# Sliding-window attention with sinks, then a gated feed-forward: half of the row-maximum shift at two places as the bias of the exponentials, the constants' load behind that of the first keys, and another order by hand

## The chip, the cores and the metric

The kernel runs on one core of a Trainium2 chip. The time is device microseconds for one execution. Five engines run their own instruction streams and wait for each other through semaphores: PE (TensorE, matrix products, with its weight loads shown as PEld), DVE (VectorE), ACT (ScalarE), POOL (GpSimd) and SP, which only issues DMAs here.

## What is computed

Attention over 4 batches, 8 heads, 768 positions, head size 64, followed by a feed-forward block on the 3072 tokens of 8 x 64 = 512 features. A query sees the 4 first keys (the sinks) and the 128 last ones.

```python
scores = scale * np.matmul(q, k.transpose(0, 1, 3, 2))
is_sink = pos[None, :] < 4
in_window = (rel >= 0) & (rel < 128)          # rel = query position - key position
scores = np.where(is_sink | in_window, scores, -1e9)
scores = scores - np.max(scores, axis=-1, keepdims=True)
a = np.exp(scores)
a = a / (np.sum(a, axis=-1, keepdims=True) + 1e-09)
attn = np.matmul(a, v)                         # then (B, S, H*D) = (3072, 512)
h = x @ w_in                                   # 512 -> 2048
g = h * (1.0 / (1.0 + np.exp(-1.702 * h)))
out = g @ w_out                                # 2048 -> 512
```

## The kernel before

**Tiles.** The 3072 tokens are 24 blocks of 128; block b belongs to batch b // 6. The blocks are worked on in the order ORDER, and the position of a block in it is its *place*: places 0 to 3 are the first blocks of the four batches (blocks 0, 6, 12, 18), which have no block before them and no sinks apart from their own keys; places 4 to 23 are the other 20. Two places make a *pair*; the feed-forward of a pair starts when both of its places are done.

**One place.** Its stages, with their lines:
- loads of queries, keys and values by POOL's DMA queue, which convert to 16 bits on the way (L255, L277, L284). The keys of place 0 alone are loaded raw by SP's queue (L263) and converted by an engine (`round16`, L266 to L271), because `CFG["hw"]` names them. A pair's queries and keys share one buffer of the ring `qkn` (4 buffers).
- transposes of queries and keys. Places 0 to 7: by PE into PSUM (`tq`, L398 and L405; for places 0 to 3 in 16 small products for each of the two, with the identity matrix out of the constants), evicted by DVE or ACT (L355, L359) into `qkT`. From place 8: by one DMA transpose for a pair (L433), issued by SP.
- scores. Places 0 to 3: a mask is written to PSUM by two products (L473, out of the constants), and the scores of the block with itself are added (L481). Later places: the scores with the own block, those with the block before (`prv`) and those with the sinks (L510); DVE copies the part of `prv` that is inside the window over the own scores (L527).
- row maximum (L537, and L554, L557 for the sinks), subtraction of it (L578, and L602 for the sinks) into `e`, and the exponential by ACT (L617) into `a`. At places 0 to 3 maximum, subtraction and exponential are done in two halves of four heads each ("fine").
- transpose of the probabilities. Places 0 to 5: by PE (`ta`, L657), evicted by DVE or ACT. From place 6: by a DMA transpose issued by SP (L682). Places 4 to 23: POOL then splits it in two by two selects (L620, L624), one for the own values and one for those of the block before.
- products with the values (`av`, L709 to L719), division by the sum (L726, L727), and the transpose of the result into `xT`: by PE at places 0 to 5 (`tx`, L745), by one DMA transpose a pair from place 6 (L758).

**Feed-forward of a pair.** `first` (L780): products with w_in into a PSUM buffer `hT`, eight of them. At the first pair, which is worked on a token block at a time, product u needs chunk u mod 4 of w_in; the gate there is a tanh by ACT (L794) and a product by DVE (L801), so that ACT doesn't have to change its table between it and the exponentials. All later pairs have the gate in one ACT instruction (L810). `second` (L834): the sum over 2048 features with w_out into PSUM; the result is evicted by ACT or DVE and written by SP's queue (L852).

**PSUM.** Rings of buffers: `mm` (3 banks; transposes, `hT`, the outputs, and part of `av`), `own` (scores, 2 banks), `pv` (2 banks; `prv`, `av`, and the own scores of places 1 and 3), `mi` (1 bank). A product can only start when a buffer of its ring has been read out.

**What sets the order.** Every operation is an entry of a plan, with engines that may take it, what it depends on, and the buffers that it takes and gives back. The order, and the engine of each operation, is not searched when the program is built: it is the string SEQUENCE, where `38d` says that entry 38 comes next and runs on DVE (p is PE, a ACT, d DVE, t POOL, s SP). Each engine executes its entries in this order and waits where an input or a buffer isn't there. The costs, transfer times and due times at the entries were used by the search that wrote the string; they don't act on the program. The entries are numbered as they are added. Numbers that the text needs: 0 load of the constants, 37 raw load of place 0's keys, 38 their conversion, 12 to 18 queries and keys of places 0 to 3, 19, 20, 23, 24 the values of places 0, 1, 2, 3, 21, 22, 25, 26 the chunks 0 to 3 of w_in, 101 to 123 place 0, 124 to 146 place 1, 147 to 169 place 2, 170 to 192 place 3 (in each: transposes and evictions first, then mask, scores, maxima, subtractions, exponentials), 197 the scores of place 4, 270, 296, 322, 348 the DMA transposes of queries and keys of places 8 and 9, 10 and 11, 12 and 13, 14 and 15.

The entry with the bias exists in the code before, for a place that `CFG["nb"]` names; before, it names none. With n halves named, the last n halves of the place get no subtraction:

```python
plan.add(DVE, ..., nc.vector.tensor_scalar(out=nbias[:, 2-nb:], in0=small[:, 2-nb:], scalar1=-scale, op0=ALU.mult))
for j in range(4):     # one ACT instruction of 128 columns for each head, straight from the scores in PSUM
    nc.scalar.activation(out=a16()[:, 512*l + P*j : 512*l + P*j + P], in_=own(l, l+1)[:, 0, j],
                         func=AF.Exp, scale=scale, bias=nbias[:, l, j : j + 1])
```

Of the kernel before, what the change touches and what calls it, by code (L numbers as in the profile page):

```python
# [27 lines left out]
PE, ACT, DVE, POOL, SP = "PE", "ACT", "DVE", "POOL", "SP"  # L28
# [1 line left out]
    tq=(0, 1, 2, 3, 4, 5, 6, 7),  # L30
    ta=(0, 1, 2, 3, 4, 5),
    tx=(0, 1, 2, 3, 4, 5),
    nb={},
    wide={1: 'pv', 3: 'pv'},
    fine=(0, 1, 2, 3),
    split=(0, 1),
    gbatch={},
    tanh=(0, 1),
    last=(256, 128, 128),
    hw=["k0"],  # L40
    big=(0, 1, 2, 3),
    avb={0: ("mi", "mm"), 1: ("mi", "mm"), 2: ("mi", "mm")},
    hb={},
# [11 lines left out]


SEQUENCE = """
0s 10d 4d 37s 12t 7d 14t 11a 16t 13t 106p 38d 15t 9d 2d 103p 6d 23t 3d 101p 104a 20t 126p 102a 18t 107p 127d 17t
124p 19t 108d 149p 109d 125a 22t 147p 150a 110d 129p 25t 148a 130p 111d 112a 105t 131d 113a 114p 132d 170p 115a 26t
116p 133d 171a 118p 152p 21t 117a 119d 153p 135a 134d 29t 120p 8d 137p 136a 121d 172p 33t 138a 154d 122p 173a 30t  # L60
139p 156d 123a 175p 155d 174t 140a 141p 481p 142d 158a 24t 157d 143p 176p 482a 144d 160p 34t 159a 483d 145p 161a 27t
177d 162p 484p 163a 146d 28t 179d 166p 487p 485a 167d 181a 486d 493p 488a 178d 489d 490p 40t 494a 180d 39t 478p 491a
495d 182a 32t 492d 183p 164p 479a 165d 499p 36t 184a 480d 185p 42t 500a 187p 195p 186d 193p 501d 48t 189p 196a 496p
190d 194a 168p 188d 497a 217p 215p 197p 169a 498d 218a 198p 191p 43t 199d 514p 192a 508p 216d 515a 200d 518p 46t
201d 509p 519a 31t 202d 239p 502p 240a 52t 203d 219p 128t 237p 221d 503p 238a 204a 520p 67t 222d 220p 510p 5d 223d
93s 504p 225d 224d 1s 242p 49t 94s 511p 151d 226a 45t 505p 512d 241p 521a 51t 506d 516p 243d 54t 524p 517a 244d 205p
525a 528p 206d 253p 245d 529a 255p 207t 522p 254d 247d 256a 246d 530p 35t 523a 227p 97t 208p 248a 228d 258p 257p
209d 270s 531p 259d 210t 230p 532p 260d 231a 229t 211p 261d 526p 249s 232t 212d 533p 527a 263d 262d 44t 233p 60t
536p 234d 264a 55t 213p 534d 537p 214d 41t 271p 538p 50t 273d 265s 235p 250t 539p 236a 274d 272p 548p 540a 296s 275d
550p 276d 57t 549a 552p 58t 277d 283p 53t 553a 544p 285d 551a 266t 554p 545a 286d 284p 251p 555a 287d 542p 61t 252d  # L70
546p 47t 288d 267p 56t 547a 556p 543a 268d 564p 289d 557a 269s 278a 558p 541s 297p 559p 299d 290a 565p 279s 300d
298p 566p 535s 301d 560p 96s 302d 291s 567p 303d 309p 304a 280t 95s 561p 311d 568a 305s 310p 578p 562d 570p 312d
579a 322s 292t 576p 98d 281p 571a 572p 66t 282d 584p 306t 313d 573a 507s 577a 513s 293p 585a 580p 294d 64t 574p 314d
581a 295s 84t 592p 575a 315d 316a 63t 307p 593p 59t 308d 586p 73t 317s 582p 72t 594p 99t 583a 587p 70t 323p 604p
325d 348s 595p 605a 326d 588p 596a 318t 324p 600p 327d 328d 589p 601a 598p 329d 65t 590d 335p 591s 78t 608p 563s
337d 62t 612p 609a 338d 69t 599a 336p 602p 613a 68t 339d 319p 603a 341d 340d 82t 606p 76t 620p 320d 607a 85t 342a
614p 100d 321s 79t 610p 361p 75t 330a 621p 343s 363d 91t 615p 611a 364d 331s 362p 616p 365d 622p 367d 366d 617p 623p
618a 632p 374s 624d 638p 636p 344t 639a 349p 637a 630p 351d 350p 626p 631a 352d 332t 345p 627a 634p 633a 346d 628p
353d 81t 640p 354d 629a 635a 333p 368a 648p 334d 642p 355d 347s 375p 356a 643p 569s 377d 641a 376p 357s 649p 378d
644p 369s 379d 650p 380d 645p 625s 656p 619s 646d 597s 381d 387p 358t 657a 400s 662p 389d 668p 663a 370t 651p 669a  # L80
359p 652a 388p 654p 360d 77t 658p 390d 74t 660p 659a 391d 80t 655a 371p 393d 392d 661a 71t 664p 372d 676p 665a 382a
373s 401p 670p 403d 647s 402p 671p 404d 394a 383s 666p 405d 677p 667a 406d 395s 672p 407d 413p 408a 673p 415d 384t
684p 674d 678p 416d 685a 409s 414p 679p 90t 417d 426s 692p 87t 680d 385p 418d 693a 396t 696p 419d 386d 686p 682p 88t
687a 397p 410t 683a 690p 697a 398d 688p 691a 399s 698p 689a 420a 694p 411p 699p 412d 695a 421s 700p 427p 675s 710p
429d 452s 712p 711a 430d 428p 701p 713a 422t 431d 720p 432d 724p 721a 702d 439p 725a 86t 433d 718p 441d 92t 716p
719a 442d 83t 440p 714p 717a 89t 423p 715a 732p 434a 424d 704p 443d 425s 445d 733p 444d 435s 722p 446a 705p 723a
681s 465p 447s 706p 467d 734p 703s 468d 466p 750p 436t 469d 735p 751a 470d 707p 736a 448t 742p 708a 746p 743a 437p
747a 738p 438d 748p 471d 739a 449p 749a 740p 472a 450d 744p 451s 453p 726p 745a 473s 455d 727p 456d 737s 454p 728p
741a 653s 457d 760p 459d 458d 752p 474t 729p 753a 460a 761p 730d 772p 762p 773a 461s 766p 763p 767a 780p 764a 770p
475p 462t 771a 768p 781a 476d 776p 769a 778p 777a 788p 779a 463p 774p 464d 782p 775a 477s 789p 765s 783p 731s 784p  # L90
790p 785p 796p 786d 791p 797a 754p 792a 808p 793s 709s 794p 787s 809a 802p 795a 755p 803a 806p 756p 807a 798p 800p
799a 757p 801a 804p 758d 822p 759s 805a 810p 816p 811p 823p 812p 824p 813p 817p 814a 825p 818p 826a 815s 828p 819p
827s 829p 820d 830p 831p 821s 832a 833a
"""


# [69 lines left out]
def kernel(  # L166
# [28 lines left out]
    plan = Plan(RING)  # L195
# [26 lines left out]
    def by(e):  # L222
        return nc.sync if e == SP else nc.scalar
# [19 lines left out]
    )  # L243

    def sw(key, cost, fn, xfer, **kw):
        return plan.add(POOL, key, cost, fn, xfer=xfer, post=0.9, **kw)

    ld, qkn = {}, {}

    def load_block(which, b, key, after=0.0):  # L250
        bb, r = divmod(b, 6)
        pair, i = divmod(PLACE[b], 2)
        src = {"q": q, "k": k, "v": v}[which][bb, :, r * P : (r + 1) * P, :].rearrange("h s d -> s h d")
        if which == "v":
            return sw(key, 0.88, lambda b=b, x=2: nc.gpsimd.dma_start(v65[:, b, :, 0:D], src), 0.88 if pair < 4 else 0.95, deps=[z_1], after=after)  # L255
        w = "qk".index(which)
        buf = qkn[pair]
        if which + str(PLACE[b]) in CFG["hw"]:
            raw = const.tile([P, H * D], FP32, name=f"raw_{which}{b}")
            n = CFG["hw"].index(which + str(PLACE[b]))  # L260
            src = {"q": q, "k": k}[which][bb, :, r * P : (r + 1) * P, :].rearrange("h (t e) d -> t h (e d)", e=8)
            got = plan.add(
                {SP: 0.45, ACT: 0.6}, -120 + n, 0, lambda e, src=src, raw=raw, x=9: by(e).dma_start(raw, src), xfer=0.75, post=0.6  # L263
            )

            def round16(e, b=b, w=w, i=i):  # L266
                dst, src = buf()[:, i, w].rearrange("p h d -> p (h d)"), raw
                if e == ACT:
                    nc.scalar.copy(out=dst, in_=src)
                else:  # L270
                    (nc.vector if e == DVE else nc.gpsimd).tensor_copy(out=dst, in_=src)  # L271

            return plan.add({DVE: 0.42, ACT: 0.6, POOL: 0.8}, -110 + n, 0, round16, deps=[got], take=[buf])
        if PLACE[b] in CFG["big"]:
            return sw(
                key, 0.64,
                lambda b=b, w=w, i=i: nc.gpsimd.dma_start(  # L277
                    buf()[:, i, w].rearrange("p h d -> p (h d)"),
                    {"q": q, "k": k}["qk"[w]][bb, :, r * P : (r + 1) * P, :].rearrange("h (t e) d -> t h (e d)", e=8),
                ),  # L280
                0.7, take=[buf], after=after,
            )
        return sw(
            key, 0.88, lambda b=b, w=w, i=i: nc.gpsimd.dma_start(buf()[:, i, w], src), 0.88 if pair < 4 else 0.95,  # L284
            take=[buf], after=after,
        )
# [4 lines left out]
    def load_w_in(f, key):  # L291
        def go(f=f, x=0):
            nc.gpsimd.dma_start(  # L293
                w_in16[:, :, bass.ts(f, 512)],
                moe_w_in.rearrange("(c p) f -> p c f", p=P)[:, :, bass.ts(f, 512)],
            )

        return sw(key, 0.8, go, 2.5)

    def load_w_out(f, key):  # L300
        def go(f=f, x=1):
            nc.gpsimd.dma_start(
                w_out16[:, bass.ts(f, 4)],
                moe_w_out[bass.ts(f, 512), :].rearrange("(c p) f -> p c f", p=P),
            )

        return sw(key, 0.8, go, 2.5)

    for n, what in enumerate(CFG["loads"]):
        w, x = what[0], int(what[1:])  # L310
        x = ORDER[x] if w in "qkv" else x
# [583 lines left out]
```

## Time and profile before

| | |
|---|---|
| runs | 229.1, 229.35, 229.35 us; median 229.35 |
| the profiled execution | 228.31 us, span from the first to the last instruction 226.6 us |
| granted TensorE clock | 1.00 in every stretch |
| busy | PE 214.5, ACT 136.6, DVE 136.2, POOL 113.5 us |
| DMA | 32.47 MB in 226.6 us |
| costliest lines | L780 (`first`) 94.1 us, L834 (`second`) 91.8 us, both PE |

Busy time of the engines by stretch, in us of the stretch:

| stretch | PE | DVE | ACT | POOL |
|---|---|---|---|---|
| 0 to 10 | 4.50 | 3.62 | 3.16 | 8.85 |
| 10 to 20 | 8.68 | 9.43 | 8.90 | 6.64 |
| 20 to 30 | 9.27 | 9.05 | 7.66 | 5.76 |
| 30 to 40 | 10.00 | 8.79 | 7.11 | 5.07 |
| 60 to 80 | 19.85 | 15.76 | 12.07 | 11.49 |
| 80 to 100 | 20.00 | 12.19 | 10.96 | 15.73 |
| 100 to 120 | 18.77 | 11.62 | 11.10 | 11.66 |
| 120 to 140 | 20.00 | 13.93 | 12.44 | 7.76 |
| 200 to 227 | 23.48 | 1.92 | 7.07 | 0.00 |

A group's line in the profile reads: code line, engine, operation, output and inputs, their shapes, the number of instructions; then busy time in us and the mean of one in ns; then the idle time of the engine just before them and what ended it. A line of the timeline reads: start, duration, engine, line, operation, and in brackets the idle time before it and what ended it.

### The profile page before, as it was taken

How to read it: one execution, taken by the hardware profiler on the slowest of the kernel's cores; microseconds unless marked ns; L12 is line 12 of the kernel's file. 1: busy time of each engine (PE TensorE's matmuls, PEld its weight loads, DVE VectorE, ACT ScalarE, POOL GpSimd, SP SyncE). 2: the span in 40 equal slices, each digit the busy share in tenths (PEclk: the TensorE clock that was granted, in tenths of full speed). 3: DMA queues.
4: the chain of work that ended last, by engine and by line, in shares of the span. 5: the costliest groups of instructions: out<-in, count | busy, mean ns of one | idle time of the engine just before them, and what ended most of it. 6: DMA issues, size and time to landing. Idle time of an engine off the chain costs nothing.

```text
span 226.6 us, 5625 instructions
## 1 busy us (share of the span) xinstructions
PE 214.5 (95%) x2378; PEld 151.7 (67%) x2378; DVE 136.2 (60%) x243; ACT 136.6 (60%) x190; POOL 113.5 (50%) x135
## 2 busy tenths in 40 slices
PE   1889899999999999999899999999999999999994
PEld 0658876776784785675675685686765956856763
DVE  0899898998896852796286677843957371111010
ACT  2588696796746766367349249848585669613511
POOL 8955654698980689397071670780816112300000
PEclk9999999999999999999999999999999999999999
DMA  6999999999999999999998998999998072042112
GB/s 128 174 205 196 178 191 191 156 142 137 134 164 157 203 210 156 120 219 134 148 174 133 260 138 144 127 147 130 150 116 198 4 191 38 17 138 77 66 46 93
DMA packets 123512, 32.47 MB, mean 143 GB/s; under 512 B 114880, under 2 KB 120416, under 8 KB 123488
## 3 DMA queue, kind: packets, MB, share of 16 engines
q0 software_dynamic: 71792, 13.51, 79.6%
q1 hardware_dynamic: 51552, 18.55, 44.7%
q8 instruction: 18, 0.29, 0.6%
q10 hardware_dynamic: 144, 0.07, 0.1%
q14 instruction: 6, 0.05, 0.1%
HBM read 27.46 MB, written 6.29 MB: 149 GB/s over the span
## 4 chain that ended last, share of the span: by engine, by line
PE 77%; DMA 10%; POOL 5%; DVE 2%; ACT 1%; SPq 1%; issue 1%; POOLq 0%; DVEq 0%
PE o L834 33%; PE hT L780 31%; DMA w_in<-in_moe_w_in_dram 6%; DMA at<-a 4%; PE own L481 3%; PE av L715 2%; PE av L719 2%; PE av L709 2%; PE prv L481 2%; POOL qkn L277 2%; SPq L682 1%; POOL v L255 1%; POOL w_in L293 1%; PE tq L405 1%; PE snk L510 1%
## 5 line engine op out<-in xcount | busy, mean ns | idle before, releaser
L780 PE MATMUL hT<-xT,w_in 128*128 128x256 f16 (+1 forms) x896 | 94.1, 257 | 1.4 <-DMA xT<-xn 0.6
L834 PE MATMUL o<-w_out,gT 128*128 128x512 f16 (+2 forms) x416 | 91.8, 363 | 0.0
L810 ACT ACTIVATE gT<-hT 128x512 f16<-128x512 f32 x88 | 50.9, 597 | 58.7 <-PE hT L780 58.4
L780 PEld LDWEIGHTS <-w_in 128*128 128x128 f16 x896 | 75.3, 98 | 14.5 <-DMA xT<-xn 1.1
L834 PEld LDWEIGHTS <-gT 128*128 128x128 f16 x416 | 37.2, 98 | 32.2
L620 POOL TENSOR_SCALAR_AFFINE_SELECT atp<-at 128x1024 f16<-128x1024 f16 (+1 forms) x22 | 22.2, 1009 | 65.7 <-DMA at<-a 64.7
L527 DVE COPY_PREDICATED own<-consts,prv 128x1024 f32<-128x1024 uint16 x20 | 24.6, 1229 | 24.3 <-PE prv L481 24.2
L537 DVE TENSOR_REDUCE mx<-own 128x8 f32<-128x1024 f32 (+1 forms) x28 | 29.7, 1068 | 0.9 <-PE own L481 0.4
L578 DVE TENSOR_TENSOR e<-own,mx 128x1024 f32<-128x1024 f32 (+1 forms) x28 | 29.8, 1066 | 0.9
L617 ACT ACTIVATE a<-e 128x1056 f16<-128x1056 f32 (+1 forms) x28 | 26.2, 952 | 4.9 <-issue 2.6
L624 POOL TENSOR_SCALAR_AFFINE_SELECT at<-at 128x1024 f16<-128x1024 f16 (+1 forms) x22 | 22.5, 1024 | 1.5
L355 DVE COPY osb<-o 128x512 f32<-128x512 f32 (+1 forms) x12 | 8.0, 666 | 24.3 <-PE o L834 24.3
L284 POOL DMA_DIRECT2D qkn<-in_k_dram x20 | 17.8, 902 | 7.4 <-DMA w_out<-in_moe_w_out_dram 5.1
L255 POOL DMA_DIRECT2D v<-in_v_dram x24 | 21.4, 902 | 0.0
L726 DVE RECIPROCAL rcp<-av 128x8 f32<-128x8 f32 (+1 forms) x28 | 5.5, 195 | 26.5 <-PE av L719 26.4
L284 POOL DMA_DIRECT2D qkn<-in_q_dram x20 | 17.8, 894 | 2.3 <-DMA qkn<-in_k_dram 0.7
L810 ACT ACT_TABLE_LOAD x14 | 18.0, 1283 | 0.2
L727 DVE TENSOR_TENSOR xn<-av,rcp 128x512 f16<-128x512 f32 (+1 forms) x28 | 17.2, 615 | 1.0
L715 PE MATMUL av<-v,at 128*128 128x65 f16 x192 | 17.0, 194 | 0.6 <-POOL at L624 0.5
L617 ACT ACT_TABLE_LOAD x13 | 16.7, 1283 | 0.2
L715 PEld LDWEIGHTS <-at 128*128 128x128 f16 x192 | 14.2, 98 | 2.5 <-POOL at L624 1.2
L481 PEld LDWEIGHTS <-qkT 64*128 64x128 f16 x352 | 10.2, 96 | 7.8 <-issue 5.1
(56 smaller groups left out, 165.9 us busy)
## 6 DMA issues: line engine op xcount, KB each, us to landing
out_dram<-osb SPq DMA_DIRECT2D x23, 256.0 KB, 2.5
qkn<-in_q_dram POOLq DMA_DIRECT2D x24, 128.0 KB, 5.3
v<-in_v_dram POOLq DMA_DIRECT2D x24, 128.0 KB, 5.6
qkn<-in_k_dram POOLq DMA_DIRECT2D x23, 128.0 KB, 8.6
w_in<-in_moe_w_in_dram POOLq DMA_DIRECT2D x4, 512.0 KB, 10.2
w_out<-in_moe_w_out_dram POOLq DMA_DIRECT2D x4, 512.0 KB, 11.6
at<-a SPq DMA_TRANSPOSE x18, 3.3
raw_k<-in_k_dram SPq DMA_DIRECT2D x1, 256.0 KB, 4.6
```

The source lines that it names most:

```text
L255: return sw(key, 0.88, lambda b=b, x=2: nc.gpsimd.dma_start(v65[:, b, :, 0:D], src), 0.88 if pair < 4 else 0.95, deps=[z_1], after=after)
L284: key, 0.88, lambda b=b, w=w, i=i: nc.gpsimd.dma_start(buf()[:, i, w], src), 0.88 if pair < 4 else 0.95,
L527: nc.vector.copy_predicated(out=own(lo, hi).rearrange("p l j s -> p (l j) s"), mask=later.unsqueeze(1).to_broadcast((P, 4 * (hi - lo), P)) ...
L537: lambda lo=lo, hi=hi, own=half, small=small: nc.vector.tensor_reduce(out=small[:, lo:hi], in_=own(lo, hi), axis=AX.X, op=ALU.max),
L578: nc.vector.tensor_tensor(out=e32()[:, 512 * lo : 512 * hi].rearrange("p (l j s) -> p l j s", j=4, s=P), in0=own(lo, hi), in1=small[:, lo: ...
L617: nc.scalar.activation(out=a16()[:, lo:hi], in_=e32()[:, lo:hi], func=AF.Exp, scale=scale)
L620: nc.gpsimd.affine_select(out=atp()[:, lo : lo + n], in_=at()[:, lo : lo + n], pattern=[[0, n], [-1, P]], compare_op=ALU.is_gt, fill=0.0, ...
L624: nc.gpsimd.affine_select(out=at()[:, lo : lo + n], in_=at()[:, lo : lo + n], pattern=[[0, n], [1, P]], compare_op=ALU.is_ge, fill=0.0, ba ...
L715: nc.tensor.matmul(acc[:, j], at()[:, c], v65[:, b, h], start=(r == 0), stop=(r == 0))
L780: nc.tensor.matmul(ht()[:, n], w_in16[:, c, bass.ts(f, P)], xt[g]()[:, tok, c], start=(c == 0), stop=(c == 3))
L810: lambda fs=fs, cols=cols, gt=gt, ht=ht: nc.scalar.activation(out=gt()[:, fs[0] : fs[-1] + 1, cols], in_=ht(), func=AF.Gelu_apprx_sigmoid),
L834: nc.tensor.matmul(po(), gt()[:, F, bass.ts(t, P)], w_out16[:, F, cols], start=(F == 0), stop=(F == NF - 1))
```

## The change

Four things:
- `CFG["nb"]` names places 2 and 3 with one half each. There, for the second half of the heads, the subtraction of the maximum by DVE (128x512) and the one exponential of 512 columns out of `e` become one DVE product of the four maxima with -scale and four exponentials of 128 columns each, out of PSUM, with that product as bias. The scores' PSUM buffer is given back by the exponentials. Entries 156 to 159 (place 2) and 179 to 182 (place 3) were: subtraction, subtraction, exponential, exponential; they are: product, subtraction of the first half, exponentials of the second half, exponential of the first half.
- SP's queue begins with the raw load of place 0's keys; the constants come second. Place 0's mask products come behind its transposes and not ahead of them.
- The whole string SEQUENCE is another one, and with it the engine of several operations.
- Costs, transfer times and due times of loads in the plan are changed. They are numbers of the search that wrote the string.

```diff
-    nb={},
+    nb={2: 1, 3: 1},
...
-    hw=["k0"],
+    hw=['k0'],
...
 SEQUENCE = """
-0s 10d 4d 37s 12t 7d 14t 11a 16t 13t 106p 38d 15t 9d 2d 103p 6d 23t 3d 101p 104a 20t 126p 102a 18t 107p 127d 17t
-124p 19t 108d 149p 109d 125a 22t 147p 150a 110d 129p 25t 148a 130p 111d 112a 105t 131d 113a 114p 132d 170p 115a 26t
-116p 133d 171a 118p 152p 21t 117a 119d 153p 135a 134d 29t 120p 8d 137p 136a 121d 172p 33t 138a 154d 122p 173a 30t
-139p 156d 123a 175p 155d 174t 140a 141p 481p 142d 158a 24t 157d 143p 176p 482a 144d 160p 34t 159a 483d 145p 161a 27t
-177d 162p 484p 163a 146d 28t 179d 166p 487p 485a 167d 181a 486d 493p 488a 178d 489d 490p 40t 494a 180d 39t 478p 491a
...
+37s 6d 0s 7d 12t 4d 16t 3d 15t 13t 10d 11a 14t 38a 17t 18t 103p 20t 101p 104a 19t 106p 102a 22t 107p 25t 124p 108d
+26t 126p 125a 8d 149p 109d 127a 21t 147p 110d 129p 148a 23t 111d 130p 150a 33t 2d 112a 131d 113a 114p 133d 105t 172p
+115a 132d 116p 152p 135a 30t 117d 173a 134d 120p 170p 29t 121d 118p 136a 137p 153p 119d 138a 139p 24t 154d 171a 122p
+141p 140a 155d 175p 151t 123a 143p 156d 176p 157d 481p 144d 158a 34t 142d 484p 177d 482a 145p 159a 9d 483d 146a 180d
+160p 485a 487p 27t 161d 182a 486d 128t 493p 178d 488a 162p 489d 494a 163d 28t 490p 495d 40t 179d 166p 164p 491a 478p
...
-        return plan.add(POOL, key, cost, fn, xfer=xfer, post=0.9, **kw)
+        return plan.add(POOL, key, cost, fn, xfer=xfer, **{"post": 1.1, **kw})
...
-                {SP: 0.45, ACT: 0.6}, -120 + n, 0, lambda e, src=src, raw=raw, x=9: by(e).dma_start(raw, src), xfer=0.75, post=0.6
+                {SP: 0.45, ACT: 0.6}, -120 + n, 0, lambda e, src=src, raw=raw, x=9: by(e).dma_start(raw, src), xfer=0.9, post=0.6
...
-                key, 0.64,
+                key, 0.56,
...
-        return sw(key, 0.8, go, 2.5)
+        return sw(key, 0.8, go, 2.5, post=2.0)
```

What the new string holds in the stretches that the prediction speaks of:

| where | before | after |
|---|---|---|
| POOL's first loads | queries of 0, keys of 1, keys of 2, queries of 1, queries of 2, values of 2, values of 1, keys and queries of 3, values of 0, then w_in chunks 1, 2, 3, 0 | queries of 0, keys and queries of 2, queries and keys of 1, queries and keys of 3, values of 1, values of 0, then w_in chunks 1, 2, 3, 0, then values of 2 |
| PE's first products | masks of 0, transposes of 0, keys of 1, scores of 0, queries of 1, transposes of 2, masks and scores of 1 | transposes of 0, masks and scores of 0, transposes of 1, transposes of 2, masks and scores of 1 |
| conversion of place 0's keys | DVE | ACT |
| ACT ahead of the first exponential | 5 evictions of queries and keys | the conversion and 6 evictions |
| evictions of `ta` of places 0, 2 and 3 | DVE has 1 of 6 | DVE has 5 of 6 |
| second copy of xT of place 1 | DVE | ACT |
| PE between `av` of place 7 and the first product of pair 3 (places 6 and 7) | 1 `first`, 2 `second`, scores of 10, 2 `second`, sinks, 3 `second`, scores of 11, 1 `second`, sinks | 2 `second`, scores of 10, 1 `first`, sinks, 3 `second` |
| PE between `av` of place 11 and the first product of pair 5 (places 10 and 11) | 1 `first`, 2 `second`, 1 `first`, scores of 15, 2 `second`, sinks, 4 `second` | 2 `second`, 1 `first`, 1 `second`, scores of 15, 1 `second`, sinks, 2 `second` |
| POOL between the selects of places 10 and 11 | 7 loads, one vsb product | 10 loads |
| POOL between the selects of places 11 and 13 | 11 loads | one copy of sink keys |

More of the change, by code (lines that the diff above doesn't have):

```diff
@@ L63 @@
[L63 to L92, printed above, removed]
@@ L93 @@
-827s 829p 820d 830p 831p 821s 832a 833a
+37s 6d 0s 7d 12t 4d 16t 3d 15t 13t 10d 11a 14t 38a 17t 18t 103p 20t 101p 104a 19t 106p 102a 22t 107p 25t 124p 108d
+26t 126p 125a 8d 149p 109d 127a 21t 147p 110d 129p 148a 23t 111d 130p 150a 33t 2d 112a 131d 113a 114p 133d 105t 172p
+115a 132d 116p 152p 135a 30t 117d 173a 134d 120p 170p 29t 121d 118p 136a 137p 153p 119d 138a 139p 24t 154d 171a 122p
+141p 140a 155d 175p 151t 123a 143p 156d 176p 157d 481p 144d 158a 34t 142d 484p 177d 482a 145p 159a 9d 483d 146a 180d
@@ new lines @@
+160p 485a 487p 27t 161d 182a 486d 128t 493p 178d 488a 162p 489d 494a 163d 28t 490p 495d 40t 179d 166p 164p 491a 478p
+167d 39t 181a 492d 183p 165d 32t 499p 479a 184d 36t 480d 185p 500a 187p 186d 195p 43t 193p 501d 189p 496p 194a 188d
+31t 196a 190d 217p 497a 215p 168p 197p 498d 169a 218a 199d 191p 514p 216a 42t 192a 200d 198p 508p 515a 518p 201d
+202d 509p 35t 519a 239p 48t 203d 237p 219p 240a 54t 220p 502p 238a 221d 204a 503p 222d 520p 46t 223d 504p 224d 510p
+225d 5d 241p 226a 93s 49t 511p 1s 521a 45t 505p 512d 73t 243d 242p 516p 506a 44t 524p 244d 517a 41t 205p 525a 528p
@@ new lines @@
+245d 206d 522p 529a 247d 246d 253p 523a 255p 530p 254d 61t 248a 256d 208p 207t 227p 270s 209d 257p 97d 531p 259d
+210t 228a 230p 532p 231a 260d 229t 258p 211p 249s 261d 526p 232t 212d 533p 527a 263d 262d 52t 233p 536p 55t 234d
+264a 213p 57t 537p 214d 51t 271p 538p 250t 273d 534a 265s 235p 539p 236a 274d 272p 548p 540a 53t 275d 552p 277d 549a
+62t 276d 296s 550p 283p 266t 553a 554p 285d 284p 542p 555a 94s 286d 551a 59t 251p 287d 544p 47t 252d 546p 58t 545a
+289d 543a 288d 267p 50t 547a 558p 278a 268d 564p 269s 297p 556p 299d 513s 298p 279s 565p 557a 300d 559p 541s 98t
@@ new lines @@
+301d 566p 507s 290a 302d 95s 60t 578p 303d 567p 304a 309p 291s 568d 280t 560p 311d 579a 305s 576p 312d 561p 577a
+281p 562a 322s 310p 570p 282d 292t 572p 313d 571a 314d 574p 65t 580p 315d 535s 575a 66t 293p 581a 584p 573a 306t
+294d 586p 585a 295s 316a 592p 74t 587p 90t 582p 64t 317s 307p 583a 69t 593p 308d 67t 588p 63t 323p 604p 70t 325d
+589p 56t 605a 326d 324p 594p 590a 79t 327d 612p 72t 328d 600p 318t 613a 335p 601a 595p 337d 348s 606p 174t 596a 329d
+338d 598p 607a 602p 336p 608p 603a 339d 599a 341d 319p 340d 609a 620p 330a 320d 614p 321s 610p 342a 615p 361p 611a
@@ new lines @@
+343s 621p 363d 362p 563s 622p 364d 591s 616p 331s 365d 638p 366d 374s 344t 617p 639a 367d 623p 618a 349p 75t 632p
+351d 597s 332t 628p 569s 633a 352d 624a 350p 634p 353d 345p 635a 84t 355d 630p 629a 346d 68t 636p 631a 88t 626p 85t
+333p 627a 91t 640p 637a 334d 78t 648p 354d 641a 347s 99t 642p 356a 81t 649p 76t 375p 650p 377d 368a 357s 643p 378d
+376p 651p 369s 379d 644p 380d 668p 625s 652d 387p 669a 619s 645p 389d 400s 358t 656p 646d 660p 657a 390d 658p 370t
+381d 662p 659a 359p 663a 83t 654p 360d 77t 664p 655a 71t 661a 388p 371p 391d 665a 82t 666p 382a 372d 670p 392d 373s
@@ new lines @@
+676p 393d 394a 401p 383s 671p 403d 667a 677p 395s 404d 402p 678p 405d 647s 672p 407d 96s 406d 679p 384t 673p 408a
+680d 413p 674d 684p 415d 396t 696p 685a 409s 416d 385p 414p 426s 686p 386d 690p 687a 397p 691a 410t 692p 697a 398d
+688p 417d 693a 399s 682p 419d 689a 418d 86t 411p 683a 80t 694p 412d 87t 698p 695a 100t 420a 427p 699p 429d 710p 430d
+700p 421s 711a 428p 701p 431d 681s 432d 716p 452s 702a 724p 439p 725a 422t 718p 717a 441d 675s 703s 712p 719a 433d
+442d 714p 713a 440p 720p 715a 443d 423p 721a 732p 434a 424d 704p 444d 722p 445d 435s 446a 733p 705p 723a 653s 425s
@@ new lines @@
+734p 465p 447s 706p 467d 436t 466p 726p 468d 735p 469d 707p 736a 471d 470d 437p 708a 448t 727p 709s 438d 746p 742p
+89t 747a 449p 92t 743a 728p 472a 450d 738p 451s 729p 739a 737s 453p 730d 473s 744p 455d 752p 745a 456d 750p 740p
+751a 454p 772p 741a 457d 753a 459d 474t 748p 458d 773a 778p 749a 760p 779a 460a 768p 761p 770p 461s 762p 771a 475p
+763p 476d 769a 766p 764a 774p 767a 776p 462t 775a 782p 777a 783p 780p 788p 781a 784p 463p 789p 464d 754p 477s 790p
+731s 785p 791p 786d 755p 792d 796p 756p 797a 802p 757p 803a 806p 758d 808p 759s 807a 793s 794p 809a 787s 765s 798p
@@ L94 @@
+795a 800p 799a 822p 801a 804p 823p 805a 810p 824p 811p 825p 816p 826d 812p 827a 817p 813p 818p 814a 828p 819p 815s
+829p 820d 830p 831p 821s 832a 833a
 """
@@ L305, in go @@
             )
-        return sw(key, 0.8, go, 2.5)
+        return sw(key, 0.8, go, 2.5, post=2.0)
     for n, what in enumerate(CFG["loads"]):
```

## The prediction

> **What bounds the kernel now.** I read the page's engine table first, then what PE waited for, then the timeline of the first 30 us, then PE's chain and SP's queue in the middle.
>
> ```profile
> span 226.6 us, 5625 instructions
> PE 214.5 (95%) x2378; PEld 151.7 (67%) x2378; DVE 136.2 (60%) x243; ACT 136.6 (60%) x190; POOL 113.5 (50%) x135
> ```
>
> PE is busy for all but 12.1 us, and the change takes no matmul away. It can only move those idle microseconds. PE's waits (total, times, longest) say where most of them are:
>
> ```profile
> PE own L473 <- DMA consts<-cconst: 2.9, 1, 2.9
> PE tq L398 <- DVE qkn L271: 2.4, 1, 2.4
> PE hT L780 <- DMA xT<-xn: 0.6, 1, 0.6
> ...
> PE av L715 <- POOL at L624: 0.5, 1, 0.5
> ```
>
> 5.3 us pass before the first transposes of queries and keys (tq), 3.1 us follow the last matmul, some 2 us are gaps between 14 and 26 us, and 1.2 us lie between 109 and 119 us (0.63 for xT, 0.53 and 0.07 for at). The start, from the timeline (start, us, engine, line):
>
> ```profile
> 5.81 0.43 DVE L271 CAST qkn<-raw_k 128x512 f16<-128x512 f32 x1 [3.94 <-DMA raw_k<-in_k_dram]
> ...
> 6.29 1.07 PE L398 MATMUL tq<-consts,qkn 128*64 128x64 f16 x32 [2.40 <-DVE qkn L271]
> ...
> 11.11 0.61 PE L481 MATMUL own<-qkT 64*128 64x128 f16 x8
> ...
> 23.45 1.96 PE L780 MATMUL hT<-xT,w_in 128*128 128x128 f16 x32 [0.56 <-DMA w_in<-in_moe_w_in_dram]
> ```
>
> The first keys land at 5.8, place 0's scores start at 8.18, place 1's at 11.11, and the first product that needs w_in chunk 0 at 23.45. From 10 to 24 us DVE is busy for 9 of 10 us: there the vector work sets the pace. At 29.58 the scores of place 4 start, and from there to 109 us PE has no wait above 0.2 us. Both orders put the same PE work ahead of place 4's scores, so their start measures the whole beginning.
>
> **The bias, L565 to L590.** For half of the heads of places 2 and 3 a subtraction and one exponential of 512 columns become a tiny product and four exponentials of 128 columns.
>
> ```profile
> L617 ACT ACTIVATE a<-e 128x512 f16<-128x512 f32 x8 | 5.0, 634 | 0.5 <-DVE e L578 0.5
> ...
> L359 ACT COPY osb<-o 128x128 f32<-128x128 f32 x2 | 0.5, 265 | 1.5 <-PE o L834 1.5
> ...
> L578 DVE TENSOR_TENSOR e<-own,mx 128x512 f32<-128x512 f32 x8 | 5.4, 683 | 0.0
> ...
> L726 DVE RECIPROCAL rcp<-av 128x4 f32<-128x4 f32 x8 | 1.4, 169 | 0.0
> ```
>
> DVE saves 2 x (0.68 - 0.17) = 1.0 us. An ACT instruction of 128 columns out of PSUM is the COPY at 0.265, so four cost 1.06, and ACT pays 2 x (1.06 - 0.63) = 0.9 us. Bounds: 4 x 0.107 (128 columns at the slope between 265 and 584 ns) gives 0.43, a gain of 0.2 each; 4 x 0.45 (halfway from 0.265 to 0.634) gives 1.8, a loss of 1.2 each. I take 1.06, the row of that shape. The Trainium skill ("ScalarE: Activation LUTs", What ACT_TABLE_LOAD costs) speaks against the edit: a bias read through a pointer adds about 93 ns to each instruction, which its formula makes some 1.27 us for four. No row here has such a bias; by the page ACT's price would be 1.3 us instead of 0.9. The new wait, exponentials for the product, stands on ACT ahead of the first tanh of place 0's feed-forward; DVE's gate product (L801), and through it a PSUM buffer of the mm ring, wait behind that.
>
> **Work handed over up to place 4.** Four evictions of transposed weights go from ACT (0.587 each) to DVE (0.420); DVE gives up the cast of the first keys (0.43), a query/key eviction (0.69) and an xT copy (0.41), which ACT does in 0.59 each. With the bias, DVE has 1.0 + 1.5 - 1.7 = 0.9 us less, ACT 0.9 + 1.8 - 2.3 = 0.3 us more.
>
> **The first keys ahead of the constants.** SP issues raw_k at 0.81 instead of 1.22, with no constants before it: landing at 5.4 if the 4.6 us from issue to landing stay, earlier by the constants' share of the queue; I take 4.9. ACT casts in 0.59: 5.5. The constants, now second, land between 3.6 (0.81 + 0.75 + their 2.05) and 5.8. So tq starts at 5.6 (5.2 to 6.3), a gain of 0.7. It doesn't last. From tq to place 0's scores it is 1.89 us in both orders (two casts on ACT; place 0's masks, at 2.86 before, now fill that gap). But place 1's keys were transposed in that gap, and now their 0.5 us stands behind it: 0.53 for the scores, 4 x 0.5 for tq, 0.97 for masks put place 1's scores at 11.0 instead of 11.11. The same row shows that PE is slow here: the mask pair takes 1.03 at 2.86 and at 10.14 and 0.59 at 12.88 at a granted clock of 1.00. By the Trainium skill ("TensorE: Matmul & The Clock Gate", What's actually happening) full rate comes after a busy window of some 3.4 us, so unbroken work from 5.6 might bring it before 12 and save up to 0.4 us. The trace agrees on the two rates.
>
> **From there to place 4.** ACT now has both evictions of place 2 and one more of place 1 ahead of place 0's first exponential: it starts when tq of place 2 ends (10.0) plus two at 0.59, 11.2 instead of 10.83. Followed through ACT's and DVE's order with the rows above, place 0's xT is done at 17.6 instead of 16.9 and the first feed-forward product starts 0.8 late. DVE, with 0.9 us less, wins this back by the w_in chunk 0 product: 23.4, as before. That chunk lands 0.7 us earlier, at 22.7, since 131 KB of place 2's values now follow it at some 190 GB/s; it is no longer the last to come, the gate product that frees a PSUM buffer is. Four tanh/gate pairs and place 3's bias follow, and place 4's scores come at 29.75: **+0.2 us**, between -0.7 (only w_in's landing counts) and +1.1 (nothing won back).
>
> **The middle.** What was added or doubled there is nothing, but transposes by DMA have new deadlines. SP's queue and PE's chain before:
>
> ```profile
> 60.69 3.54 SPq L433 DMA_TRANSPOSE qkT<-qkn  x1
> ...
> 67.83 2.39 SPq L758 DMA_TRANSPOSE xT<-xn  x1
> ...
> 90.26 5.67 SPq L433 DMA_TRANSPOSE qkT<-qkn  x1
> 101.22 1.24 SPq L758 DMA_TRANSPOSE xT<-xn  x1
> ```
>
> ```profile
> 69.43 0.33 PE own L481 x8
> ...
> 76.11 2.64 PE hT L780 x24
> ```
>
> The transpose for places 10 and 11 landed 8.3 us after its issue, 69.0, and place 10's scores ran at 69.43: 0.4 to spare. In the new order one feed-forward product (0.87) that stood ahead of them stands behind, so they are wanted at 68.56, while its last load still goes out fourth in a row: **+0.4** (0 to 2). xT of places 6 and 7 landed 5.7 us after its issue, 73.5, wanted at 76.11. Now from place 7's output at 66.83 there are only 1.73 + 0.55 + 0.87 + 0.09 + 2.6 = 5.85 us of PE work ahead of its first reader: 72.7, or 73.1 behind the former stall: **+0.4** (0 to 3, if it took the 8.4 us of the third such transpose). For places 14 and 15, POOL before made seven loads and a vsb product in a row ahead of place 11's selects; now ten loads, with the sixth of them (out at 84.2 + 5 x 0.9 = 88.7, place 10's selects ending some 1.3 late) needed by the transpose. That goes out at 93 to 97 instead of 90.26, takes the 9.6 us of before, and is wanted at about 104: 0 to 2.6. xT of places 10 and 11 has 6.7 us of PE work ahead of its reader where it had 9.4 and was still 0.63 late; without loads beside it I give it the median 5.3 instead of 8.4, plus 1.0 to 1.6 for the division: 0 to 3. The two share what they stall: **+0.9**. Against this, no burst of loads precedes place 13's transpose any more (its at took 10.0 us), and the old 1.23 us go: **-1.2**.
>
> The rest costs nothing: sink keys, vsb products and z_s move to POOL and DVE stretches with an idle half, hidden by PE's matmuls; the output writes moved on SP are waited for by none but SP. If SP is held by one, at or xT issues behind it are late by its 0.5 us. The final products and evictions keep their order. The planner's cost edits set no instruction.
>
> **Sum:** 0.2 + 0.4 + 0.4 + 0.9 - 1.2 = +0.7. The profiled execution took 228.31 (span 226.6, 1.7 around it): 229.0. The median of the runs, 229.35, lies 1.04 above it, so **230.1**, with a range of its own from 229.6 to 232.2.
>
> **Rivals.** (1) *The start pays and the deadlines hold* (0.28). DVE's relief carries through until w_in's landing sets the pace, -0.7, the old 1.2 us go, and at most 0.3 come back: 229.35 - 1.6 = 227.8. For it: DVE's 9 tenths from 10 to 24 us. Against it: ACT gets the work. It decides if place 4's scores start before 29.2 and PE waits under 0.6 us from 60 to 120. (2) *Wins and losses cancel* (0.17): start -0.2, old stalls gone, 1.4 of new: 229.35. (3) *A transpose cascades* (0.10): a transpose that takes the 10 us of place 13's holds SP's queue and the next at is late too: 1.2 + 2 more, 232.6. (4) *The bias isn't what it says*: a row of 128-column exponentials at 0.43 a set would give back 1.3 us of ACT; within (1).
>
> **Chances.** The forecast has 0.45. Faster by over 0.2% (0.46 us, about what these runs tell from no change): (1) and a little of (2), 0.30. Within: the rest of (2) and the forecast's low edge, 0.18. Slower: 0.52. The range, 228.2 to 232.2, cuts off the better half of (1) and most of (3).
>
> **What would show it.** Raw_k's cast ending at 5.5 and on ACT; place 1's scores within 0.3 of 11.0; four exponentials at 1.06 together; place 4's scores at 29.5 to 30; PE waiting for qkT near 69 and 104 and for xT near 73 and 107; no wait for at near 115. I am wrong if place 4 comes a microsecond earlier, or if transposes land in 3 to 5 us where I count 6 to 10.

## The result and the profile after

The changed kernel takes 234.84 us (median of four runs, 233.77 to 236.82) where the kernel before takes 229.35: 1.0272 of it, with a 95% interval of 1.0232 to 1.0312. The profiled execution took 233.77 us. The prediction had the sign, by luck as the sum below shows, and missed the size: 230.1, with 232.2 as the upper end.

The engine table and PE's waits of the kernel after, to be read against those of before (waits: total us, times, longest):

```profile
span 232.1 us, 5629 instructions
PE 215.8 (93%) x2378; PEld 152.9 (66%) x2378; DVE 131.3 (57%) x237; ACT 141.2 (61%) x201; POOL 114.7 (49%) x138
```

```profile
PE tq L398 <- DMA consts<-cconst: 5.5, 1, 5.5
PE av L715 <- POOL at L624: 4.1, 2, 3.7
PE ta L657 <- ACT a L617: 0.9, 1, 0.9
PE ta L657 <- ACT xT L359: 0.8, 1, 0.8
```

The span grew by 5.5 us and PE's busy time by 1.3 us with the same number of products: some of them ran slower. The second wait line is new: 3.7 us in one piece, where no wait after 30 us was above 0.63 before. It ends at 54.73, at the products of place 4's probabilities with the values. POOL's timeline around it, of after:

```profile
42.66 1.78 POOL L255 DMA_DIRECT2D v<-in_v_dram  x2
52.35 0.88 POOL L284 DMA_DIRECT2D qkn<-in_k_dram  x1 [7.91 <-DMA qkT<-qkn]
53.34 0.63 POOL L620 TENSOR_SCALAR_AFFINE_SELECT atp<-at 128x512 f16<-128x512 f16 x1
```

and of before:

```profile
51.14 0.63 POOL L620 TENSOR_SCALAR_AFFINE_SELECT atp<-at 128x512 f16<-128x512 f16 x1
51.84 0.64 POOL L624 TENSOR_SCALAR_AFFINE_SELECT at<-at 128x512 f16<-128x512 f16 x1
52.43 0.93 POOL L255 DMA_DIRECT2D v<-in_v_dram  x1
53.91 0.87 POOL L284 DMA_DIRECT2D qkn<-in_q_dram  x1 [0.56 <-DMA qkT<-qkn]
```

A load into a query/key buffer waits in both for the DMA transpose that reads what the buffer held. In the built programs place 13's pair gets the memory of the pair of places 8 and 9, and not that of the older pair of places 6 and 7, whose transposes PE had done by 46.9 us. Before, that load (60t, queries of place 13) stands behind the selects of places 4 and 5 and waits 0.56 us that nobody needs. After, the first of that pair's loads (61t, keys of place 13) stands ahead of them. The chain of waits of after, cut to this stretch (start, us, what):

```profile
40.93 6.05 DMA qkn<-in_q_dram
46.98 0.02 SPq L433
...
47.04 4.75 DMA qkT<-qkn
...
52.35 0.06 POOL qkn L284
...
53.34 0.64 POOL atp L620
...
56.02 0.23 PE av L715
```

A load of 6.05 us, a transpose of 4.75 behind it, then the issue of a load whose data the transpose of its pair takes only at 84, then the selects, then PE. Then comes a second loss. Busy time by stretch, of after (PE, PEld, DVE, ACT, POOL with instructions, then the granted clock, DMA share, GB/s):

```profile
50.00:53.00 3.00, 1.08 (x10) 0.47 (x7) 1.66 (x4) 1.91 (x3) 0.65 (x1) 1.00 0.93 194
53.00:54.00 1.00, 0.00 (x0) 0.00 (x0) 0.00 (x0) 0.00 (x0) 0.85 (x2) 0.64 0.04 9
54.00:60.00 6.00, 4.82 (x38) 3.40 (x39) 2.13 (x4) 1.60 (x2) 5.76 (x9) 0.50 0.34 22
60.00:61.00 1.00, 1.00 (x21) 0.80 (x19) 0.11 (x1) 0.99 (x2) 1.00 (x2) 0.95 1.21 78
```

While PE stood, its clock fell to half, and the first 5.4 us of its new work ran at 0.50: 16 products of `first` took 1.89 us instead of 1.05, 4 of `second` 1.91 instead of 1.03. From 62 to 200 us PE has no wait of note.

### The profile page after: what moved, and what is told of

The parts are those of the page before. It is cut to its first block, busy times and chain, and to the rows that moved or that the text cites. A ratio compares the mean times of both kernels' runs of the same rounds, so it can differ in the third digit from the quotient of the medians.

```text
span 232.1 us, 5629 instructions
## 1 busy us (share of the span) xinstructions
PE 215.8 (93%) x2378; PEld 152.9 (66%) x2378; DVE 131.3 (57%) x237; ACT 141.2 (61%) x201; POOL 114.7 (49%) x138
## 4 chain that ended last, share of the span: by engine, by line
PE 72%; DMA 18%; POOL 6%; issue 1%; DVE 0%; ACT 0%; POOLq 0%; SPq 0%
PE hT L780 31%; PE o L834 31%; DMA w_out<-in_moe_w_out_dram 6%; DMA w_in<-in_moe_w_in_dram 6%; DMA qkn<-in_q_dram 3%; PE av L715 2%; DMA xT<-xn 2%; PE own L481 2%; PE av L719 2%; DMA qkT<-qkn 2%; PE av L709 2%; POOL qkn L277 2%; PE prv L481 1%; POOL qkn L284 1%; POOL w_in L293 1%
## 5 line engine op out<-in xcount | busy, mean ns | idle before, releaser
L834 PE MATMUL o<-w_out,gT 128*128 128x512 f16 (+2 forms) x416 | 92.9, 365 | 0.0
L780 PEld LDWEIGHTS <-w_in 128*128 128x128 f16 x896 | 76.3, 99 | 14.3 <-DMA w_in<-in_moe_w_in_dram 0.9
L578 DVE TENSOR_TENSOR e<-own,mx 128x1024 f32<-128x1024 f32 (+1 forms) x26 | 28.4, 1095 | 0.7
L617 ACT ACTIVATE a<-e 128x1056 f16<-128x1056 f32 (+1 forms) x26 | 25.0, 981 | 1.6 <-DVE e L602 1.3
L355 DVE COPY osb<-o 128x512 f32<-128x512 f32 (+2 forms) x11 | 6.9, 629 | 20.6 <-PE o L834 20.5
## 6 DMA issues: line engine op xcount, KB each, us to landing
w_in<-in_moe_w_in_dram POOLq DMA_DIRECT2D x4, 512.0 KB, 10.5
```

The source lines that it names most:

```text
L578: nc.vector.tensor_tensor(out=e32()[:, 512 * lo : 512 * hi].rearrange("p (l j s) -> p l j s", j=4, s=P), in0=own(lo, hi), in1=small[:, lo: ...
L617: nc.scalar.activation(out=a16()[:, lo:hi], in_=e32()[:, lo:hi], func=AF.Exp, scale=scale)
L780: nc.tensor.matmul(ht()[:, n], w_in16[:, c, bass.ts(f, P)], xt[g]()[:, tok, c], start=(c == 0), stop=(c == 3))
L834: nc.tensor.matmul(po(), gt()[:, F, bass.ts(t, P)], w_out16[:, F, cols], start=(F == 0), stop=(F == NF - 1))
```

## The experiments

Ratios are to the kernel before on the same chip, with 95% intervals. Profiles are of one execution each.

**The load moved behind the selects** (e1_load_behind).

```diff
-... 254d 61t 248a 256d 208p 207t ... 232t 212d ...
+... 254d 248a 256d 208p 207t ... 232t 61t 212d ...
```

> The changed kernel with one instruction moved: the load of place 13's keys (61t), which stands ahead of the selects of places 4 and 5 on POOL, goes behind them. Theory A (the load waits for the transpose of pair 4, holds POOL from about 50 to 52.35 and so the selects; PE idles 3.65 us and then works for some 5 us at half clock): place 4's tx comes at about 54 us instead of 61.55, and the time falls by 6 to 7.4 us, to 227.5 to 228.8 (the median before is 229.35, after 234.84). Rival B (the loss is spread over the new order or comes with the bias): it stays above 233. Rival C (the deadlines of the prediction near 69, 73, 104 and 107 us bite as soon as PE is no longer late): the stall goes, but PE waits 1 to 1.7 us there and the time is 229 to 230.5.

228.75 us, 1.0012 (0.9987 to 1.0036). POOL no longer waits for a transpose there, and place 4's transposed output (`tx`) comes at 55.08 instead of 61.55. One instruction's place accounts for the whole loss; rival B falls. PE's waits show part of rival C:

```profile
PE hT L779 <- DMA xT<-xn: 0.7, 1, 0.7
PE av L714 <- DVE at L354: 0.7, 1, 0.7
PE av L714 <- POOL at L623: 0.5, 1, 0.5
```

The first is xT of places 6 and 7 at 74.4, one of the four waits predicted; the third is at 80.1; the second lies in the start.

**Five buffers, the order untouched** (e2_five_buffers).

```diff
-RING = dict(qkn=4, ...
+RING = dict(qkn=5, ...
```

> The changed kernel, its order untouched, with five query/key buffers instead of four, so that place 13's pair need not wait for pair 4's. Theory A: POOL's wait for qkT<-qkn ahead of the selects (7.9 us) goes, the selects start at 50 to 51, and the time is that of the kernel with the load moved, within 1 us (227.5 to 229.5). If it is the place of the load in POOL's queue by itself that costs (0.9 us of issue): 233 to 235, as after.

227.88 us, 0.9965 (0.9940 to 0.9990). The load still stands ahead of the selects, issues at 44.49 and waits for nothing:

```profile
44.49 0.92 POOL L284 DMA_DIRECT2D qkn<-in_k_dram  x1
45.52 0.63 POOL L620 TENSOR_SCALAR_AFFINE_SELECT atp<-at 128x512 f16<-128x512 f16 x1
```

It is the wait and not the place that costs. PE's waits of this run, from 29 us on, are two of 0.2:

```profile
PE hT L780 <- ACT gT L810: 0.2, 1, 0.2
PE tx L745 <- DVE gT L801: 0.2, 1, 0.2
```

**The same mistake made in the kernel before** (e3_before_ahead).

```diff
-... 207t ... 233p 60t 536p ...
+... 60t 207t ... 233p 536p ...
```

> The kernel before with only its own waiting load (60t, place 13's queries; it waited until 53.9 behind the selects) moved ahead of place 4's first select. Theory A: POOL stands until the transpose of pair 4 has landed, the selects start 3 to 4 us late, the granted clock falls, and this one move costs most of what the whole change cost: 3.5 to 7 us, 233 to 236.5. Rival B: 229.3 to 230.3.

237.71 us, 1.0403 (1.0366 to 1.0439): 9.2 us, more than expected. POOL waited 9.0 us for the transpose, and PE this long:

```profile
PE av L708 <- POOL vsb L333: 6.5, 1, 6.5
PE own L480 <- DMA qkT<-qkn: 1.3, 1, 1.3
```

The size was off because POOL in that order has more between the load and the values: a select pair, a load and the product for the sinks' values (`vsb`, 1.14 us) come first, so PE's first product starts at 57.69 instead of 50.31. Half clock behind it (0.50 from 55 to 61) and later transposes add to that. The mechanism is shown without any other part of the change.

**The wait kept, the clock kept up** (e4_keep_warm).

```diff
+            for _ in range(13 if PLACE[b] == 4 else 0):
+                nc.tensor.matmul(bank(lo), ident, w_out16[:, 0, :], start=True, stop=True)
             for l in range(lo, hi):
```

> The changed kernel with 13 products of 128x512 that nobody reads (about 3.4 us at 0.26) put on PE just ahead of place 4's attention times values, into its accumulator, where PE only waits. The selects are as late as after. If half of the loss is the clock that falls after the idle time: the clock stays at 1.00 from 54 to 60, 16 hT products take 0.93 instead of 1.89 and 4 o products 1.03 instead of 1.91, and 2 to 3 us come back: 231.8 to 233. If the wait alone is the loss: 234 to 235.5.

231.8 us, 1.0169 (1.0116 to 1.0221), against 1.0272 with the clock falling: 1.0% or 2.4 us back. POOL is as late (52.31), PE is not slowed. Stretches of this run:

```profile
53.00:54.00 1.00, 0.97 (x5) 0.29 (x3) 0.00 (x0) 0.00 (x0) 0.83 (x2) 1.00 0.05 10
54.00:60.00 6.00, 4.53 (x64) 3.23 (x65) 3.03 (x6) 2.62 (x3) 5.78 (x9) 1.00 0.35 24
```

The 13 products took 2.97 us out of a wait that was there anyway, and `tx` of place 4 came at 59.70 instead of 61.55 (timelines of this run, then of after):

```profile
50.90 2.97 PE L707 MATMUL av<-w_out,consts 128*128 128x512 f16 x13
...
59.70 0.39 PE L747 MATMUL tx<-consts,xn 128*128 128x128 f16 x4
```

```profile
61.55 0.39 PE L745 MATMUL tx<-consts,xn 128*128 128x128 f16 x4
```

With `tx` at 55.0 without the stall, 6.5 us of delay divide into 1.85 for the clock and 4.7 for the wait. Useless work made the kernel faster than none. The rest of the 2.4 us wasn't followed up; one of the four runs took 234.67 us, the others 231.64 to 231.85.

**The kernel before with five buffers** (e5_before_five; the same edit of RING).

> The kernel before with five query/key buffers instead of four, order untouched. The changed order with five buffers ran at 0.9965 of before. If that small gain is the new order's: this kernel stays within 0.2% of before, since its own loads of pair 6 waited only 0.56 us, behind the selects, where no matmul stood on them. If it is the fifth buffer's: 0.996 to 0.998 here too, and the new order is worth nothing.

228.4 us, 0.9972 (0.9943 to 1.0002). No gain is shown, but the median lies where the fifth buffer was expected to put it if the gain is its own, and the interval allows up to 0.6%. So this run doesn't settle what the fifth buffer is worth in the old order. Its profile has a wait of 1.6 us for xT of a pair where before had 0.6.

**No bias, five buffers** (e6_no_bias; `nb={}` and the entries 156 to 159 and 179 to 182 in the kinds and order of before).

> The changed kernel with five buffers and without the bias: places 2 and 3 subtract the maximum on DVE for all heads, as before, the rest of the order unchanged. By the prediction's rows the bias takes 1.0 us from DVE and gives ACT 0.9 to 1.3, in the stretch from 10 to 26 us where both are full. If DVE sets the pace there, place 4's scores come 0.3 to 0.8 us later than 29.18 and the time rises by as much, to 0.998 to 1.000 of before; if ACT does, they come 0.2 to 0.6 earlier and it is 0.994 to 0.996; if they balance, it is within 0.1% of 0.9965.

228.29 us, 0.9968 (0.9937 to 0.9999), level with the 0.9965 that the same kernel with the bias had in its first measurement; its second, below, is 0.9928 (0.9901 to 0.9956). Place 4's scores came at 29.39, inside the 29.06 to 29.76 of the six runs with the bias and this start. No effect of the bias is shown. A gain of some 0.4% from the bias, the distance to the second measurement, isn't ruled out, since the intervals overlap.

**Only the first keys ahead of the constants** (e7_keys_first, in the order of before).

```diff
-0s 10d 4d 37s 12t ... 106p 38d 15t 9d 2d 103p 6d 23t 3d 101p 104a
+37s 0s 10d 4d 12t ... 38d 15t 9d 2d 103p 6d 23t 3d 101p 106p 104a
```

> The kernel before with only the load of the first keys issued ahead of the constants, and place 0's masks, which need the constants, moved behind the transposes of its queries and keys on PE. Theory: tq starts at 5.5 instead of 6.29, waiting for the constants now; the masks fill what follows; of the 0.7 us no more than 0.3 is left at place 4's scores (29.2 to 29.6 instead of 29.52), since vector work sets the pace from 10 us on: 0.998 to 1.000. Rival: PE, at work without a break from 5.5, gets its full rate by 9.5 as in the changed kernel, and 0.4 to 0.7 us stays: 0.997 to 0.998.

227.98 us, 0.9962 (0.9930 to 0.9994). In its profile tq started at 5.29 and the masks of place 1 ran at full rate at 9.58, as the rival had it; but place 4's scores came at 29.84, later than either theory. The stretches tell why:

```profile
11.00:12.50 1.50, 0.40 (x4) 0.23 (x4) 1.50 (x4) 1.21 (x3) 1.14 (x2) 1.00 1.63 202
12.50:15.00 2.50, 2.49 (x34) 1.58 (x34) 1.38 (x4) 1.65 (x3) 1.86 (x3) 0.52 1.22 201
```

PE had got ahead of ACT and of a load, worked 0.4 of 2 us, and its clock fell again. So this execution lost in the start what it had won, and the small gain of the median isn't explained by it. That stays open.

**Both mends** (e8_five_behind).

> The changed kernel with both mends: five buffers, and place 13's keys behind the selects of places 4 and 5. With four buffers and the load behind, PE waited 0.71 us for xT of places 6 and 7 at 74.4 and 0.47 for selects at 80.1; with five and the load ahead it waited for neither. If the later load is what collides there: the stalls come back, and it is 1.000 to 1.002 of before. If it was the buffer (loads of pair 6 and 7 held up behind one another): no stalls, 0.995 to 0.998.

228.72 us, 0.9997 (0.9971 to 1.0022), with 0.6 us of wait for xT of places 6 and 7. A later load of place 13's keys beside that transpose would explain it, but the kernel without the bias has the load early and waited 1.3 us there. In these profiles, one execution each, the wait is 0, 0, 0.6, 0.7 and 1.3 us, and its cause isn't settled. In time, both kernels with the load behind the selects (1.0012 and 0.9997) lie above the three with five buffers and the load ahead (0.9928, 0.9965 and 0.9968), so the later load may cost something in itself; no run isolates that.

**Keys first and five buffers in the old order, beside the new order with five buffers again** (e9_keys_first_five, e10_five_again; one chip).

> The kernel before with the first keys ahead of the constants and five query/key buffers, its order otherwise untouched. If the two add (0.9962 and 0.9972 alone): about 0.993 to 0.995, better than the changed order with five buffers (0.9965), and the rest of the new order is worth nothing or less. If both are the same noise around a small gain: 0.995 to 0.999, level with the changed order.

> The changed kernel with five buffers once more, on the same chip as the run beside it: 0.994 to 0.999 of before by the first measurement. If the searched order in the middle is worth something over keys first and five buffers, it is at least 0.2% below the run beside it.

228.72 us, 0.9980 (0.9948 to 1.0012), and 227.61 us, 0.9928 (0.9901 to 0.9956). The two gains don't add. The changed kernel with five buffers is below the kernel before in both measurements, by 0.35% and 0.72%; it is faster than the kernel before, by less than 1%, and than the changed kernel with four buffers. That it also beats the old order with the same two edits (by 0.5% here) isn't settled: these intervals overlap, and the old order with either edit alone lay at 0.9972 and 0.9962, level with the first measurement of the new order (0.9965).

## Why the prediction was wrong

**The step that failed** is "The rest costs nothing". I followed POOL through the first 30 us and between the selects of places 10, 11 and 13, but not ahead of the selects of places 4 and 5, where a load moved past them. The trace of before had the price: a load that waits for the transpose of places 8 and 9 until 53.91, in a queue that executes in order, and products of place 4 with the values that PE starts at 50.3. With the load ahead, 0.87 for its issue and 1.3 for one pair of selects bring the first of them to 56.1, 5.7 us late. In the kernel after, with the transpose 2 us earlier, POOL's part of PE's waits is 4.1. The wait was hard to see because it was only 0.56 us long: it was short because of its place.

**The clock was not in the sum at all.** It multiplied the wait by 1.4: 1.85 us on 4.7. The prediction spoke of the clock for the start alone.

**The sum, term by term**, as far as the runs show it:

| term | predicted | measured |
|---|---|---|
| start, by place 4's scores | +0.2 | 29.06 to 29.76 in six runs, mean 29.34; three runs with the start of before 29.27, 29.52 (29.58 in the prediction), 30.02, mean 29.60: -0.3 |
| transpose of places 10 and 11 | +0.4 | 0 in five runs without the stall |
| xT of places 6 and 7 | +0.4 | 0, 0, 0.6, 0.7 and 1.3: mean 0.5 |
| transpose of 14 and 15, xT of 10 and 11 | +0.9 | 0 in five |
| the old stalls | -1.2 | gone in the five; in the old order the wait for xT isn't fixed: 0.6, 1.6 with five buffers, none with the first keys ahead |
| load ahead of the selects | not seen | +6.5 |

The changed kernel with five buffers has a span of 225.7 us, 0.9 below before; with the 6.4 us from there to 232.1 that is the +5.5 of the two profiles. Without the last row the measured terms add up to -1.0, where +0.7 was predicted: the forecast of a slower kernel came true through a term that wasn't in it, which is luck.

**The start.** The keys' cast ended at 5.2 on ACT (predicted 5.5), tq started at 5.48 (5.6), the constants being last, and place 0's scores at 7.45 (7.5). For place 1's scores 11.0 was predicted: 10.69 and 10.93 in the two runs where the masks ahead of them still took 1.03 us, 10.02 in the profile of after, where they took 0.60:

```profile
5.48 1.06 PE L398 MATMUL tq<-consts,qkn 128*64 128x64 f16 x32 [5.48 <-DMA consts<-cconst]
...
9.48 0.60 PE L473 MATMUL own<-consts 128*128 128x512 bf16 x2
10.02 0.40 PE L481 MATMUL own<-qkT 64*128 64x128 f16 x8
...
16.26 1.91 PE L780 MATMUL hT<-xT,w_in 128*128 128x128 f16 x31
```

What I put beside the sum as a remark, the earlier full rate, was the larger effect in this profile: the first `hT` came at 16.26, 0.7 early, and not 0.8 late. But w_in's landing still ends the wait ahead of chunk 0's product (at 22.37, predicted 22.7), and much of such a lead is lost there: in the seven runs with the changed start the first `hT` lie 1.5 us apart (15.80 to 17.32) and this product 0.7 (22.37 to 23.09). Against before this product came 1.1 us earlier, place 4's scores only 0.5.

**The bias.** Four exponentials took 1.14 us in both places (predicted 1.06 from the 265 ns of a copy; the estimate from the formula of the Trainium skill, "ScalarE: Activation LUTs", What ACT_TABLE_LOAD costs, was 1.27):

```profile
16.59 1.14 ACT L590 ACTIVATE a<-own,nb 128x128 f16<-128x128 f32 x4 [0.45 <-DVE e L578]
23.97 1.14 ACT L590 ACTIVATE a<-own,nb 128x128 f16<-128x128 f32 x4
```

So ACT pays 2 x (1.14 - 0.63) = 1.0 and DVE saves 2 x 0.68 - 0.46 = 0.9: the sizes were right to 0.1 us, and the two still balance.

**The DMA deadlines.** I gave the transposes the durations that they had had among other loads, 8.3 and 9.6 us. SP's queue of the run with the load moved:

```profile
63.59 1.64 SPq L432 DMA_TRANSPOSE qkT<-qkn  x1
68.79 1.35 SPq L757 DMA_TRANSPOSE xT<-xn  x1
...
98.56 2.84 SPq L432 DMA_TRANSPOSE qkT<-qkn  x1
104.03 1.54 SPq L757 DMA_TRANSPOSE xT<-xn  x1
```

From issue to landing these took 3.7 us (places 10 and 11; scores at 69.37), 5.5 (places 6 and 7, 0.7 late) and 4.9 (places 14 and 15). The last went out later than I had counted (93 to 97), landed at 103.5 and was wanted at 106.3. That "transposes land in 3 to 5 us where I count 6 to 10" stood under what would make me wrong, and two of three did.

**The rivals.** Rival 1 (the start pays, the deadlines hold) gave 227.8, 0.993 of before. Once the load no longer waits, the change comes to 0.9965 and 0.9928 with five buffers, near it, but to 1.0012 with the load moved, where PE waited 1.2 us in the middle. Its marks were there in the profile of after, place 4's scores at 29.06 and no wait of PE from 62 on, where PE was 6.5 us late; the mean of six runs, 29.34, misses its 29.2. Rival 3 had the right kind of mechanism, a transpose that holds a queue in order, at 232.6, but put it on SP's queue.

## What to carry to other kernels

When an order changes, list for each queue that executes in order every instruction that waits for a buffer, and look at what it has moved past; a wait of half a microsecond in the old trace can be eight in another place, and the time at which it ended is the figure to carry over, not its length. If PE stands for some 2 us or more in the middle of a kernel, as in the three cases below, ask what half clock behind it would cost. A ring with one more buffer is a cheap test of such a wait, and here the mend with the lower time (0.9965 and 0.9928 against 1.0012).

## What the runs showed of the hardware

**The clock falls sooner than I had expected.** After the change PE's last product ended at 51.07, and the mean of 0.64 between 53 and 54 puts the fall at 53.3: 2.2 us. In the kernel before with the load ahead it was 51.16 and 54.5, 3.3 us. With the first keys ahead 2.1 us with 0.4 us of work in them were enough (10.5 to 12.6). The Trainium skill ("TensorE: Matmul & The Clock Gate", What's actually happening) gives an idle window of some 3.4 us that runs freely. The free run agrees with the spread, but all three falls came before 3.4 us of standing, and in the 3.4 us ahead of them PE had worked some 1.2, 0.1 and 1.7 us: such a window need not be empty. Full clock came back 5.4, 3.6 and 3.5 us after work began again. From fall to full clock it was 6.8, 6.8 and 3.4 us (53.3 to 60.1, 54.5 to 61.3, 12.6 to 16.0), two, two and one such windows.

**Full rate at the start came at different times.** In seven runs with the changed start tq began between 5.02 and 5.48, and place 1's scores between 9.59 and 10.93, according to when the rate rose. It had risen by 9.05 in the run with the clock kept up, where place 1's masks took 0.61 us; in the run with both mends 16 products of tq at 12.27 still took 0.64 us, and not the 0.44 of the others. The granted clock in the profile reads 1.00 in this stretch in all of them, also where the mask pair takes 1.03 us and not 0.60: before the first rise it doesn't show the half rate.
